# Spans of 256 steps, 384-byte packets, 64x64 array tiles and weights prepared among the attention steps in a gated linear attention + MoE kernel

## Chip, cores, metric

One core of one Trainium2 chip. The metric is the device time of one launch in microseconds (us); lower is better.

## The reference, cut

```python
# attention: B=4, H=8, S=768, D=48
f = 1 / (1 + exp(-f_logit))
for t in range(S):
    state = f[:, :, t, :, None] * state + einsum('bhd,bhe->bhde', k[:, :, t], v[:, :, t])
    y[:, :, t] = einsum('bhd,bhde->bhe', q[:, :, t], state)
# MoE: x = y as (3072 tokens, 384); w1, w2: 384 x 1024; w_out: 1024 x 384
out = maximum(x @ w1, x @ w2) @ w_out
```

Both kernels use max(a, b) = b + relu(a - b). So the output is x·(w2·w_out) + relu(x·(w1 - w2))·w_out. The matrix `m2` = w2·w_out and the difference `wd` = w1 - w2 (rows permuted) are computed once at the start on the chip. Attention is done in chunks: decays become exponentials of cumulative sums, and inside a chunk it is products of matrices.

## The kernel before

It works on tiles of 128 steps of one batch: 24 tiles, two tiles form a token group of 256 for the MoE. The stages have one-letter names, which the rest of the text uses. SBUF and PSUM are the on-chip memories in which the tiles lie (results of TensorE land in a bank of PSUM), and a semaphore is the counter by which one engine waits for another:

| letter | engine | what |
|---|---|---|
| E | ScalarE | `ell` = ln(1 + exp(-f)) |
| C, X | TensorE, ScalarE | cumulative sums `cum`; exponentials `f_inv`, `f_dec`, `f_last` |
| M, V | GpSimd (or VectorE) | k' = k·f_inv (`kp`), q' = q·f_dec (`qp`); v to bf16 (`vb`) |
| T | TensorE, VectorE | transposes of k', q' (`trp`), copied to SBUF (`trs`) |
| A | TensorE, VectorE | scores (`at`), masked (`at_m`) |
| S, Y | TensorE, ScalarE | y from the state, y from the scores (`y`), copied to `xT` |
| D, N | TensorE, VectorE, GpSimd | sums for the next state (`sadd`) and the new state |
| d | TensorE, ScalarE | h = x·wd (24 matmuls), relu to `gT` |
| o | TensorE, VectorE | x·m2 + gT·w_out (22 matmuls), out |

```python
def load(n, names="fkqv"):                       # 192-byte packets: 48 floats
    t = inp.tile([C, H, D], F32, ...)
    nc.sync.dma_start(out=t, in_=sources[nm][b, :, c*C:(c+1)*C, :].rearrange("h p d -> p h d"))
def stage_T_pe(n):                               # 8 transposes, 128x128
    for x, nm in enumerate(("kp", "qp")):
        for j in range(NP):
            nc.tensor.transpose(out=ps[:, x, j, :], in_=src[:, 2*j:2*j+2, :]..., identity=ident)
def stage_A_pe(n):                               # 8 products on two row halves of the array
    for j in range(NP):
        for r in range(2):
            rows = slice(r*DP, r*DP + D)
            nc.tensor.matmul(out=ps[r][:, j, :], lhsT=t[rows, 0, j, :], rhs=t[rows, 1, j, :], ...)
# ... start: tiles 0-3, then weights, wd ahead of the first d, m2 behind it ...
while n < n_tiles + 2 or queue["d"] or queue["o"]:
    do("A", n); do("Y", n - 1); do("C", n + 2); do("M", n + 2); next_piece("d", n)
    do("V", n + 1); do("T", n + 1); next_piece("d", n); do("E", n + 3); next_piece("o", n)
    n += 1
# ... cut: constants, stages E, C, X, M, V, Y, D, pieces d and o, weights
```

## Time and profile before

| | before |
|---|---|
| time, median (lowest to highest of the runs beside the new kernel) | 175.56 us (174.80 to 175.78) |
| span in the profile | 173.1 us |
| TensorE busy / idle | 140.5 / 32.6 us |
| mean granted clock of TensorE | 0.99 |
| first h matmul | 37.26 us |
| one round of 128 steps, steady | 5.05 us (10.1 per 256) |

"Busy" is the time in which an engine executes; idle is the span less busy. The granted clock says at what share of full speed TensorE was allowed to run. The lines of this profile that carry the argument stand in the prediction; two more from its page's slices (40 equal parts of the span) are needed later, the granted clock in tenths and the transfer rate in GB/s:

```profile
PEclk9999999999699999999999999999999999999999
GB/s 116 195 215 399 399 290 183 202 187 186 188 179 7 95 81 206 132 156 195 139 210 179 188 233 194 214 168 233 212 189 220 157 155 45 57 49 57 45 95 93
```

There is one dip of the clock. (The trace's record of the clock begins at 37.3 us, and what lies before is counted as full; the weight matmuls just before, 512 columns each, start 0.43 us apart, against 0.23 in e6, so TensorE ran at about half clock there too. The new kernel's record begins at 15.2 us, that of its repeat at 31.3. So means of the clock over whole runs are not quite comparable; the stretches after the first h are.) Where DMA is busy with the 192-byte input packets, it moves around 190 GB/s; the 399 are the weights.

### The profile page before, as it was taken

The page shows a single profiled execution, that of the slowest core. Times are in us where ns is not written, and L with a number is a line of the kernel's source. Part 1 is how long each engine was busy: PE and PEld are TensorE (multiplying, and loading weights), DVE is VectorE, ACT ScalarE, POOL GpSimd, SP SyncE. Part 2 cuts the span into 40 slices and gives each one's busy share as a digit, 9 for nine tenths or more (in the row PEclk, how much of TensorE's full clock was granted, in tenths as well). Part 3 has the DMA queues.
Part 4 walks back from the last instruction along what each step waited for, and adds up shares of the span by engine and source line. Part 5 has one row for each costly group of instructions (what it writes and reads, how often), then busy time and mean ns, then how long its engine had stood idle before and what let it go on. Part 6 is the DMA issues. An engine that isn't in the chain of part 4 may idle for free.

```text
span 173.1 us, 4159 instructions
## 1 busy us (share of the span) xinstructions
PE 140.5 (81%) x1636; PEld 97.8 (56%) x1637; DVE 88.4 (51%) x168; ACT 94.4 (55%) x205; POOL 64.4 (37%) x79
## 2 busy tenths in 40 slices
PE   0157461694969958699999999999999999999992
PEld 0034250252436647567777777777777777766760
DVE  8119239410058976555467655556765554542121
ACT  4263570159234676966848396684949665343410
POOL 2078008700004465636535345652634564000000
PEclk9999999999699999999999999999999999999999
DMA  6999999999990449689799899979989741111122
GB/s 116 195 215 399 399 290 183 202 187 186 188 179 7 95 81 206 132 156 195 139 210 179 188 233 194 214 168 233 212 189 220 157 155 45 57 49 57 45 95 93
DMA packets 106772, 29.18 MB, mean 169 GB/s; under 512 B 100736, under 2 KB 105984, under 8 KB 106752
## 3 DMA queue, kind: packets, MB, share of 16 engines
q1 hardware_dynamic: 105216, 28.32, 80.6%
q10 hardware_dynamic: 1536, 0.59, 1.5%
q8 instruction: 13, 0.21, 0.5%
q14 instruction: 7, 0.06, 0.1%
HBM read 23.59 MB, written 4.72 MB: 164 GB/s over the span
## 4 chain that ended last, share of the span: by engine, by line
PE 66%; DMA 9%; DVE 8%; ACT 6%; SPq 6%; issue 2%; ACTq 1%
PE h L275 18%; PE o L285 17%; PE o L282 6%; DMA kt<-in_k_dram 5%; SPq L71 5%; PE trp L176 4%; PE at_e L194 4%; PE y L221 4%; PE y L216 3%; DMA w_f<-in_moe_w_dram 3%; PE wdp L312 3%; PE m2n L326 3%; DVE wdn L305 3%; PE cum L143 3%; ACT wo L322 2%
## 5 line engine op out<-in xcount | busy, mean ns | idle before, releaser
L163 POOL TENSOR_TENSOR kp<-kt,f_inv 128x384 bf16<-128x384 f32 x24 | 26.0, 1082 | 51.0 <-ACT f_inv L156 40.3
L275 PE MATMUL h<-xT,wd 128*128 128x256 bf16 x288 | 38.1, 272 | 0.1
L285 PE MATMUL o<-wo,gT 128*128 128x384 bf16 x192 | 35.1, 326 | 0.0
L288 DVE COPY ob<-o 128x384 f32<-128x384 f32 x24 | 13.3, 556 | 41.6 <-PE o L285 41.6
L277 ACT ACTIVATE gT<-h 128x512 bf16<-128x512 f32 x48 | 28.0, 610 | 8.9 <-PE h L275 8.5
L275 PEld LDWEIGHTS <-wd 128*128 128x128 bf16 x288 | 25.9, 98 | 3.9 <-issue 1.0
L260 ACT CAST xT<-y 128x512 bf16<-128x512 f32 x24 | 14.0, 583 | 22.0 <-PE y L221 21.8
L285 PEld LDWEIGHTS <-gT 128*128 128x128 bf16 x192 | 18.8, 98 | 12.4
L165 POOL TENSOR_TENSOR qp<-qt,f_dec 128x384 bf16<-128x384 f32 x24 | 25.0, 1043 | 0.1
L184 DVE COPY trs<-trp 128x1024 bf16<-128x1024 bf16 x24 | 16.5, 688 | 12.3 <-PE trp L176 12.3
L251 POOL TENSOR_TENSOR state<-tmp_s,f_last 128x256 bf16<-128x256 f32 x16 | 10.6, 662 | 29.8 <-DVE tmp_s L250 24.7
L156 ACT ACTIVATE f_inv<-cum 128x384 f32<-128x384 f32 x24 | 11.8, 491 | 16.7 <-POOL state L251 8.1
L202 DVE TENSOR_TENSOR at_m<-at_e,ut 128x512 bf16<-128x512 f32 x24 | 16.4, 682 | 2.0 <-PE at_o L194 2.0
L143 PE MATMUL cum<-ell,ut 128*128 128x384 bf16 x24 | 8.6, 359 | 10.6 <-ACT ell L137 10.6
L202 DVE TENSOR_TENSOR at_m<-at_o,ut 128x512 bf16<-128x512 f32 x24 | 16.3, 679 | 0.0
L136 ACT ACTIVATE tmp_e<-ft 128x384 f32<-128x384 f32 x24 | 12.8, 532 | 6.4 <-DMA ft<-in_f_logit_dram 6.4
L282 PE MATMUL o<-m,xT 128*128 128x384 bf16 x72 | 15.6, 326 | 0.0
L194 PE MATMUL at_e<-trs 48*128 48x128 bf16 x96 | 9.9, 226 | 4.0 <-DVE trs L184 3.7
L137 ACT ACTIVATE ell<-tmp_e 128x384 bf16<-128x384 f32 x24 | 12.6, 523 | 0.8
L169 DVE CAST vb<-vt 128x384 bf16<-128x384 f32 x24 | 11.4, 475 | 2.6 <-DMA vt<-in_v_dram 2.6
L146 PEld LDWEIGHTS <-ell 128*128 128x128 bf16 x96 | 6.1, 100 | 11.1 <-issue 9.8
L194 PEld LDWEIGHTS <-trs 48*128 48x128 bf16 x192 | 5.7, 97 | 11.2 <-DVE trs L184 5.9
(51 smaller groups left out, 178.0 us busy)
## 6 DMA issues: line engine op xcount, KB each, us to landing
ft<-in_f_logit_dram SPq DMA_DIRECT2D x24, 192.0 KB, 4.1
kt<-in_k_dram SPq DMA_DIRECT2D x24, 192.0 KB, 4.6
qt<-in_q_dram SPq DMA_DIRECT2D x24, 192.0 KB, 4.6
vt<-in_v_dram SPq DMA_DIRECT2D x24, 192.0 KB, 4.2
out_dram<-ob SPq DMA_DIRECT2D x24, 192.0 KB, 3.0
w_f<-in_moe_w_dram SPq DMA_DIRECT2D x6, 512.0 KB, 6.1
wo_f<-in_moe_w_out_dram SPq DMA_DIRECT2D x2, 768.0 KB, 9.2
xT<-xT ACTq DMA_DIRECT2D x24, 24.0 KB, 3.6
```

What stands on the lines that cost most here:

```text
L143: nc.tensor.matmul(out=ps[:, 0:HD].rearrange("p (h d) -> p h d", h=H), lhsT=ut, rhs=ell[:, :, 0:D], start=True, stop=True)
L163: nc.gpsimd.tensor_mul(padded["kp"][n % NB][:, :, 0:D], loaded[n]["k"], f_inv.rearrange("p (h d) -> p h d", h=H))
L165: nc.gpsimd.tensor_mul(padded["qp"][n % NB][:, :, 0:D], loaded[n]["q"], f_dec.rearrange("p (h d) -> p h d", h=H))
L184: nc.vector.tensor_copy(t, ps)
L194: nc.tensor.matmul(out=ps[r][:, j, :], lhsT=t[rows, 0, j, :], rhs=t[rows, 1, j, :], start=True, stop=True)
L202: nc.vector.tensor_mul(m[:, r], ps[r], ut4)
L260: nc.scalar.copy(xT[g][:, :, b * C:(b + 1) * C], ys.pop(n))
L275: nc.tensor.matmul(out=ps[:, f, :], lhsT=wd[:, kt, ff * C:(ff + 1) * C], rhs=xT[g][:, kt, :], start=(kt == 0), stop=(kt == KT - 1))
L277: nc.scalar.activation(gT[g][:, 2 * fp:2 * fp + 2, :], ps, AF.Relu)
L282: nc.tensor.matmul(out=ps, lhsT=xT[g][:, kt, b * C:(b + 1) * C], rhs=m2[:, kt, :], start=(kt == 0), stop=False)
L285: nc.tensor.matmul(out=ps, lhsT=gT[g][:, ff, b * C:(b + 1) * C], rhs=wo[:, ff, :], start=False, stop=(ff == FG - 1))
L288: nc.vector.tensor_copy(ob, ps)
```

## The change

The intent: half as many packets of twice the size, attention products that fill all four 64x64 quarters of the array, and TensorE kept busy at the start by attention work while weights arrive. A span is now 256 steps with steps 2p and 2p+1 on partition p; one span is one token group. The diff, cut to its core:

```diff
-            t = inp.tile([C, H, D], F32, name=f"{nm}t", tag=f"{nm}t")
-            nc.sync.dma_start(out=t, in_=...[b, :, c * C:(c + 1) * C, :].rearrange("h p d -> p h d"))
+            t = inp.tile([C, H, 2, D], F32, name=f"{nm}t", tag=f"{nm}t", bufs=in_bufs[nm])
+            src = ...[b, :, w * W:(w + 1) * W, :].rearrange("h (p two) d -> p h (two d)", two=2)
@@ transposes: 64 small ones per span in place of 16
+                for par in range(2):
+                    for r in range(2):
+                        for h in range(2):
+                            rows = slice(h * HC, (h + 1) * HC)
+                            nc.tensor.transpose(out=ps[h][r * DP:(r + 1) * DP, x, j, par, :],
+                                                in_=src[rows, par, 2 * j + r, :], identity=ident[rows, rows])
@@ scores, state sums, y: same four-quarter loops (32, 32, 32 small matmuls); one drain and semaphore
+            nc.tensor.drain().then_inc(s_sem, 1)      # between y from the state and y from the scores
@@ order of the start
+    do("AD", 0) ... weights_w2(0); do("Y", 0); weights_w2(1); do("DAN", 1); weights_w2(2); weights_wo()
+    do("S", 1); weights_m2(); do("Y", 1)
+    weights_wd()                                   # w1 - w2 on VectorE only here
@@ order of spans 2 to 6, the ramp into the regular rounds
+    do("E", 2); do("d", 0); do("CXM", 2); do("E", 3); do("o", 0); do("VT", 2); do("d", 1)
+    do("DAN", 2); do("CXM", 3); do("E", 4); do("o", 1); do("VT", 3); do("CXM", 4)
+    do("S", 2); do("D", 3); do("Y", 2); do("AN", 3); do("E", 5); do("VT", 4); do("CXM", 5); do("E", 6)
@@ regular round
+    for s in range(4, n_s + 2):
+        T(s+1) S(s-1) D(s) Y(s-1) A,N(s) d(s-2) C,X,M(s+2) V(s+1) E(s+3) C,X,M(s+3) E(s+4) o(s-2)
```

(`do` runs a stage once, so in later rounds only what is left of the list is issued: C, X, M of span s+3, E of s+4.)

## The prediction

> **What bounds the kernel now.** I read the page first, then the chain of waits in order of time, then the timeline of one round in the steady part, then that of the start. The busy table and the slices:
>
> ```profile
> PE 140.5 (81%) x1636; PEld 97.8 (56%) x1637; DVE 88.4 (51%) x168; ACT 94.4 (55%) x205; POOL 64.4 (37%) x79
> ...
> PE   0157461694969958699999999999999999999992
> ...
> DMA  6999999999990449689799899979989741111122
> ```
>
> TensorE is full from about 65 us on, and half empty before. DMA is busy nearly everywhere too, but the chain from 77.6 us on consists of TensorE alone. The busy table of the stretches says the same:
>
> ```profile
> 36.00:50.00 14.00, 10.99 (x59) 6.36 (x58) 1.20 (x3) 8.02 (x12) 0.00 (x0) 0.88 1.42 187
> 50.00:78.00 28.00, 22.70 (x351) 16.75 (x350) 21.08 (x40) 17.54 (x43) 13.91 (x15) 1.00 0.60 116
> ...
> 77.60:153.00 75.40, 75.35 (x990) 55.16 (x989) 44.82 (x89) 48.98 (x114) 35.69 (x41) 1.00 0.84 172
> ```
>
> So 75.35 of 75.40 us are TensorE: transfers are hidden there, and only TensorE time counts. It takes 5.05 us per 128 steps. Where they go, from the timeline of one such round:
>
> ```profile
> 102.15 0.41 PE L221 MATMUL y<-at_m,vb 128*64 128x128 bf16 x8
> 102.40 0.29 PE L234 MATMUL sadd<-vb,kp 128*64 128x64 bf16 x8
> 102.62 0.34 PE L143 MATMUL cum<-ell,ut 128*128 128x384 bf16 x1
> 102.80 0.24 PE L146 MATMUL cum<-ones_col,ell 128*128 128x1 bf16 x4
> 102.90 0.82 PE L275 MATMUL h<-xT,wd 128*128 128x256 bf16 x6
> 103.55 0.39 PE L176 MATMUL trp<-ident,kp 128*128 128x128 bf16 x4
> 103.78 0.39 PE L176 MATMUL trp<-ident,qp 128*128 128x128 bf16 x4
> 104.00 0.82 PE L275 MATMUL h<-xT,wd 128*128 128x256 bf16 x6
> 104.66 0.65 PE L282 MATMUL o<-m,xT 128*128 128x384 bf16 x3
> 105.14 1.46 PE L285 MATMUL o<-wo,gT 128*128 128x384 bf16 x8
> 106.54 0.23 PE L194 MATMUL at_e<-trs 48*128 48x128 bf16 x1
> ```
>
> Matmuls overlap, so I take distances between starts: h 12 x 0.109 = 1.31, o 11 x 0.163 = 1.79, together 3.1 us that the change leaves alone; cum 0.28, transposes 0.45, the scores A (to 106.87) 0.33, y from the state (to 107.21) 0.34, y from the scores 0.24, sadd 0.22: attention 1.86 us.
>
> The start, from the timeline: the first h matmul is at 37.26 us, after the subtraction w1 - w2 (26.62 to 31.7) and twelve matmuls at 0.43; m2 is ready at 51; the regular rounds begin there and still lose 5.3 us (28.0 - 22.7) before 78.
>
> **What the Trainium skill says.** "TensorEngine Tiling (Array Packing)", Key Properties: changing the tiling mode drains TensorE. The trace agrees: eight score matmuls in pairs 56 ns apart need 0.22 us but the next group starts after 0.33; eight sadd at 13.6 ns are 0.11 but cum starts after 0.22. About 0.11 us per change, four changes in a round. "TensorE: Matmul & The Clock Gate", Part 3: tiles in different row or column groups overlap, starting about 4 ns apart. The trace shows pairs only: the two score halves start within 10 ns. No run yet shows four at once. The same page, Part 1: an idle window of about 3.4 us puts the clock back to half. The trace fits: m2n matmuls run 0.32 us apart after an idle stretch, though the equally long o ones take 0.163. "DMA: Bandwidth & Descriptors", Specifications: line rate needs 512 B or more. Packet medians in this trace: 192 B 15 ns, 512 B 27, 4096 B 159, so about 8.2 ns plus 0.0368 ns per byte; 384 B come to an estimated 22.3 ns.
>
> **Part 1, packets.** Inputs are 18.9 MB. Before: 98304 packets x 15.2 / 16 engines = 93 us of transfer; after: 49152 x 22.3 / 16 = 68.5. The gain of 25 us lies beside a full TensorE, so it is worth nothing in the steady part. At the start two spans (3.15 MB) take 11.4 us at 275 GB/s where 1.57 MB took nearly 8, so weights still end near 25 us. Value by itself: about zero.
>
> **Part 2, 64x64 tiles, per 256 steps.** Before: 2 x 1.86 = 3.72. After, if four tiles run at once (four of 128 columns per 56 ns, four of 64 per 27 to 28): transposes 64 = 16 x 0.028 = 0.45 (0.90 before); state product 16 on the two diagonal tiles, 8 x 0.056 = 0.45; state sums 32 = 0.22; y from scores 32 = 0.45; scores 32 = 0.45. Products and sums take the array time they took. cum grows: four matmuls of 384 columns in place of two, 0.65, and eight of two columns at 0.025, 0.20, sum 0.85. Mode changes fall from eight to two, plus one explicit drain with its semaphore: 0.4 in place of 0.9. Sum 3.27; MoE is still 6.2; a span takes 9.5 us against 10.1. Some nine steady spans: 5 to 6 us won. The other engines fit below 9.5: ScalarE, by distances of starts (384 columns 0.375, 512 0.5): E 1.7, X 1.7, y copies 1.05, relu 2.1, two DMA issues 1.2 = 7.8; VectorE 6.2; GpSimd 4 x 0.95 + 2 x 0.66 = 5.1.
>
> **Part 3, the start.** I followed the instruction order of the new kernel by hand. f of span 0 lands at 3.9, E0 to 5.65, cum (half clock) to 7.5, exponentials to 9.2; k' on GpSimd and q' on VectorE share time (w1 - w2 took 2.01 us per part beside GpSimd, 1.21 alone), to 11; transposes, cum of span 1, scores, masks to 16.9 on VectorE; q' of span 1 after them, to 18.2; its transposes 18.7; y of span 0 to 21.3; then on ScalarE in order: copy of y and DMA issues to 23.6, two w2 casts to 25.6, two wo casts to 28.5. So m2n can start at 28.5 and is done about 33.5, m2 at 35.6. Only then does VectorE subtract w1 - w2 (3 x 1.2, to 39.2), with TensorE idle; thirteen wd matmuls, at first cold, end near 43.5. The first h comes **6 us later** than before, but with m2 and two spans (four old tiles) finished.
>
> **Part 4, the ramp.** A span's chain from cum to transposes is long: exponentials 0.9, then 2 x 1.9 on GpSimd, 5.1 us with the cum. Where the new order puts little on TensorE between, it waits: before the transposes of span 2 (o of 3.6 us between) 1.8, of span 3 1.0, of span 4 2.4, of span 5 (straight behind its cum, which itself waits for E) 5, and before cum 7, behind exponentials 6 and E7, 3.7. Near 14; I take 13, as some of the distances are pessimistic.
>
> **The sum.** 43.5 to the first h; MoE 12 x 6.2 = 74.4; attention of ten spans 10 x 3.3 = 33; stalls 13; last copy and 384 KB out 4 (3.3 for 192 KB before): 167.9 us of span. The time is 2.7 above the span (175.76 - 173.1): **170.6 us**, 3% faster.
>
> **Rivals.** (a) *Issue of small tiles becomes the bound.* TensorE gets 2781 matmuls in place of 1636. The fastest sustained start distance seen is 13.6 ns (sadd). If that is a floor per instruction rather than two tiles sharing, transposes take 0.85 and sums 0.43: +0.6 a span, all gain of part 2 gone, 177 us. For it: every matmul has its own weight load. Against it: loads and matmuls in the trace start two at a time, then pause 27 ns, as tile time would make them. (b) *The ramp swallows it.* If k' and q' are slowed by VectorE, as at 26 to 32 us before, each wait grows by 1 to 2 us, idle gaps above 3.4 us halve the clock, and the time is 174 to 176. (c) *The start is better than my chain.* If m2n runs at full clock and the wd preparation overlaps more, h comes at 38 to 39 and the time is near 165. (d) *Transfers bound the old kernel more than I think.* DMA share 0.84 while TensorE is full speaks against it; then 25 us would come off, which I don't expect.
>
> **Range and chances.** The steady part is safe to about +-3 us unless (a) holds; start and ramp each to +-4. An order this hand-laid was probably arranged to avoid some waits I see, which pulls down; (a) and (b) pull up. Range 163.5 to 177.0. Faster by over 2% means below 172.2, only 1.6 above my figure: 0.60; within 2% 0.34; slower 0.06.
>
> **What would show it.** Right: steady spans of 9.4 to 9.6 us with TensorE full; transposes of a span in 0.5 us; first h near 43; idle TensorE before the transposes of span 5 and cum 7; DMA share near 0.6 in the steady part. Wrong: transposes near 0.9 us (rival a); TensorE waiting for VectorE or GpSimd in every span (then an engine that I count as having slack sets the pace); first h before 39 (rival c); a steady span above 10 us.

## The result and the profile after

| | before | after |
|---|---|---|
| time, median (range), 4 runs each | 175.56 (174.80 to 175.78) | 181.24 (180.59 to 182.09) |
| span in the profile | 173.1 | 179.0 |
| TensorE busy + idle | 140.5 + 32.6 | 140.3 + 38.7 |
| mean granted clock, as recorded | 0.99 | 0.91 (four runs: 0.89 to 0.94) |
| first h | 37.26 | 43.37 |
| 256 steps, steady | 10.1 | 9.73 |

The ratio is 1.033 (95%: 1.028 to 1.039): the new kernel is slower. A ratio here is the mean time of one kernel's fast runs over that of the other's fast runs of the same rounds, so it isn't quite the ratio of the medians in the table.

The new kernel's page: busy times, and the slices of TensorE, clock, DMA and rate.

```profile
PE 140.3 (78%) x2780; PEld 99.5 (56%) x2781; DVE 90.0 (50%) x168; ACT 88.5 (49%) x169; POOL 55.8 (31%) x56
...
PE   0355649839979664379299999999999999999990
...
PEclk9999557987999997556969999999999999999999
DMA  6999999999039499999553959620202020202022
GB/s 150 261 261 379 378 383 244 265 261 254 13 93 277 112 268 242 239 273 209 145 120 97 267 154 241 163 98 4 101 2 93 15 95 11 96 8 97 2 92 88
```

Each digit is 4.5 us. From the 21st digit on (90 us) TensorE is full, as planned. Before it there is a hole of seven digits, and under most of it the clock reads 5 to 7. DMA is nearly idle in the last third. The busy table by stretch (length, then busy time and number of instructions of TensorE, its weight loads, VectorE, ScalarE, GpSimd; then granted clock, DMA share, GB/s; the share adds up packet times, which overlap, so it can exceed 1):

```profile
43.37:64.07 20.70, 16.94 (x310) 11.99 (x308) 9.13 (x15) 12.95 (x25) 8.05 (x5) 1.00 0.60 138
64.07:75.45 11.38, 5.85 (x201) 4.17 (x192) 6.44 (x11) 7.14 (x16) 6.33 (x5) 0.75 1.09 250
...
81.00:95.31 14.31, 10.85 (x70) 6.64 (x68) 3.24 (x7) 8.98 (x19) 8.01 (x5) 0.79 0.64 140
95.31:124.50 29.19, 28.75 (x703) 21.73 (x702) 18.06 (x33) 18.78 (x39) 13.83 (x12) 1.00 0.59 157
```

The last line is three regular rounds: 28.75 of 29.19 us busy at full clock. From the first h to there, 51.94 us, TensorE idles 14.0 us, and for half of the time after 64 us it runs at half clock. One regular round, as the timeline shows it (start, duration of the group, engine, line, operands, count):

```profile
105.05 0.45 PE L218 MATMUL trp<-ident,kp 64*64 64x64 bf16 x32
105.32 0.43 PE L218 MATMUL trp<-ident,qp 64*64 64x64 bf16 x32
...
106.60 0.64 PE L295 MATMUL y<-at_m,vb 64*64 64x128 bf16 x32
107.07 0.62 PE L235 MATMUL at<-trs 48*64 48x128 bf16 x32
107.63 2.79 PE L349 MATMUL h<-xT,wd 128*128 128x256 bf16 x24
...
111.11 0.65 PE L359 MATMUL o<-m,xT 128*128 128x384 bf16 x3
...
114.78 0.41 PE L218 MATMUL trp<-ident,kp 64*64 64x64 bf16 x28
```

Distances of starts (the lines left out start the state product at 105.57 and cum at 110.26): transposes 0.52, state product, sums and drain 1.03, y 0.47, scores 0.56, h 2.63, cum 0.85, o 3.67; sum 9.73. The 64 small transposes take little more than half of what 16 large ones took (0.90). And the waits of TensorE from the first h to the regular rounds (sum, times, longest):

```profile
PE trp L218 <- POOL qp L201: 4.2, 4, 1.6
PE cum L175 <- ACT ell L166: 3.9, 2, 3.5
PE trp L218 <- POOL kp L201: 3.8, 2, 2.9
```

So the tiles work and the start comes when predicted. Where did the time go? Busy plus idle says: 5.9 us more span are 6.1 us more idle and 0.2 us less busy. That last figure is a sum of two: the experiments below (e1, e7) show the same instructions at 136.0 us busy when the clock stays up. So about 4.5 us of work were removed as hoped, and 4.3 us came back, most of it as half clock.

When did the clock drop? The changes of clock lie on a grid of 3.41 us. The busy table cut on that grid:

```profile
66.40:69.81 3.41, 1.43 (x75) 0.92 (x63) 3.07 (x6) 2.12 (x6) 3.41 (x3) 1.00 1.21 249
69.81:73.22 3.41, 2.27 (x44) 1.47 (x44) 1.65 (x3) 1.59 (x4) 0.83 (x1) 0.50 0.99 246
...
86.87:90.29 3.42, 1.17 (x14) 0.78 (x14) 0.00 (x0) 2.25 (x6) 3.41 (x2) 1.00 1.05 247
```

After a window with 1.43 us of work, and again after one with 1.17, the next runs at half clock (the last column but two; 90.29 to 93.70 reads 0.50 like the second line). The waits need not be long each: in the first of these windows none is over 0.89 us. And half clock does not last for one window alone: the windows from 69.81 us on, with 2.27, 0.64 and 2.69 us of work, were each followed by another at half clock, and only after the one with 3.41 us (80.05 to 83.46) was it full again.

### The profile page after: what moved, and what is told of

Same layout as the page of the kernel before. It is cut to its first block, busy times and chain, and to the rows that moved or that the text cites. A ratio compares the mean times of both kernels' runs of the same rounds, so it can differ in the third digit from the quotient of the medians.

```text
span 179.0 us, 6262 instructions
## 1 busy us (share of the span) xinstructions
PE 140.3 (78%) x2780; PEld 99.5 (56%) x2781; DVE 90.0 (50%) x168; ACT 88.5 (49%) x169; POOL 55.8 (31%) x56
## 4 chain that ended last, share of the span: by engine, by line
PEld 17%; issue 15%; ACT 11%; PE 9%; ACTq 5%; POOL 4%; PEldq 3%; DVE 0%; POOLq 0%
ACT gT L351 7%; PEld L362 6%; ACTq L336 5%; ACT xT L333 3%; POOL qp L201 3%; PE o L362 3%; PEld L349 3%; PE y L295 3%; PEldq L256 3%; PEld L218 2%; PEld L276 2%; PEld L359 2%; PE h L349 1%; PE at L235 1%; PE o L359 1%
## 5 line engine op out<-in xcount | busy, mean ns | idle before, releaser
L201 POOL TENSOR_TENSOR kp<-kt,f_inv 128x768 bf16<-128x768 f32 x12 | 21.8, 1813 | 42.4 <-ACT f_inv L193 39.9
L247 DVE TENSOR_TENSOR at_m<-at,mask 128x512 bf16<-128x512 f32 x48 | 29.8, 684 | 2.9 <-PE at L235 2.4
L333 ACT CAST xT<-y 128x512 bf16<-128x512 f32 x24 | 12.9, 593 | 32.6 <-PE y L295 32.6
L175 PE MATMUL cum<-ell,u_inc 128*128 128x384 bf16 x36 | 11.3, 372 | 10.4 <-ACT ell L166 10.2
L201 POOL TENSOR_TENSOR qp<-qt,f_dec 128x768 bf16<-128x768 f32 x10 | 18.5, 1846 | 0.0
L218 PE MATMUL trp<-ident,kp 64*64 64x64 bf16 x384 | 5.9, 203 | 9.7 <-POOL kp L201 8.1
L165 ACT ACTIVATE tmp_e<-ft 128x768 f32<-128x768 f32 x12 | 10.6, 880 | 4.8 <-DMA ft<-in_f_logit_dram 3.5
L193 ACT ACTIVATE f_dec<-cum 128x384 f32<-128x384 f32 x24 | 10.8, 523 | 0.0
L166 ACT ACTIVATE ell<-tmp_e 128x768 bf16<-128x768 f32 x12 | 10.1, 843 | 0.4
L218 PE MATMUL trp<-ident,qp 64*64 64x64 bf16 x384 | 5.9, 206 | 5.5 <-POOL qp L201 4.2
L295 PE MATMUL y<-at_m,vb 64*64 64x128 bf16 x384 | 8.5, 234 | 1.5 <-PEq L256 0.2
```

The costliest lines, as they stand in the source:

```text
L193: nc.scalar.activation(t[:, pt, :], ps[pt][:, 0:HD], AF.Exp, bias=0.0, scale=scale)
L201: eng.tensor_mul(pad(nm + "p", s)[:, :, :, 0:D], by_parity(loaded[s][nm]), t.rearrange("p two (h d) -> p two h d", h=H))
L218: nc.tensor.transpose(out=ps[h][r * DP:(r + 1) * DP, x, j, par, :], in_=src[rows, par, 2 * j + r, :], identity=ident[rows, rows])
L247: nc.vector.tensor_mul(m[:, r, 2 * jj:2 * jj + 2], ps[r], mask.rearrange("p j a b t -> p j a (b t)"))
L295: nc.tensor.matmul(out=ys[s][h][r * DP:(r + 1) * DP, j, :], lhsT=vb[rows, par, 2 * j + r, :], rhs=m[rows, r, j, par, :], start=first, stop ...
L333: nc.scalar.copy(x[:, :, :, h, :], ps.rearrange("p j (a t) -> p j a t", a=2))
```

## The experiments

All twelve gave correct results. Theory "ramp": the loss lies in the order of the start and of spans 2 to 7, which leaves TensorE waiting and so also lowers its clock; tiles, packets and spans are sound. Rival "tiles": the small tiles are slower than the large ones they replaced. Rival "packets": they don't help, or the loads of 384 KB come too late. Ratios are to the kernel before on the same chip. "After" had 1.033 in its first runs. Medians are of all four runs; e1, e2 and e5 have one slow run each and e8 has two, which the ratios leave out.

| run | what | median us (range) | ratio (95%) |
|---|---|---|---|
| e1 | new order of the ramp | 167.73 (166.36 to 169.37) | 0.951 (0.948 to 0.955) |
| e2 | unread work in the longest gap | 181.45 (180.57 to 184.18) | 1.034 (1.029 to 1.039) |
| e3 | large transposes | 184.96 (183.76 to 186.51) | 1.056 (1.049 to 1.063) |
| e4 | 192-byte packets | 185.70 (184.14 to 186.59) | 1.059 (1.052 to 1.065) |
| after again | unaltered | 182.32 (180.11 to 182.77) | 1.040 (1.033 to 1.047) |
| e5 | unread work in two gaps | 182.70 (182.06 to 185.50) | 1.044 (1.038 to 1.049) |
| e6 | w1 - w2 earlier | 177.22 (176.92 to 177.43) | 1.013 (1.009 to 1.018) |
| e7 | e1 + e6 | 164.08 (163.16 to 165.20) | 0.939 (0.933 to 0.945) |
| e8 | e7, E of span 7 later | 162.52 (160.74 to 164.21) | 0.917 (0.913 to 0.922) |
| e9 | e7 with large transposes | 164.65 (164.25 to 165.66) | 0.939 (0.935 to 0.944) |
| e10 | e7 with 192-byte packets | 181.05 (180.39 to 182.26) | 1.032 (1.027 to 1.037) |
| e11 | 100 unread instructions early | 187.79 (one run) | none |

### e1: the order of the ramp

```diff
-    do("S", 1); weights_m2(); do("Y", 1); weights_wd(); do("E", 2); do("d", 0)
-    do("CXM", 2); do("E", 3); do("o", 0); do("VT", 2); do("d", 1); do("DAN", 2); do("CXM", 3); do("E", 4)
-    do("o", 1); do("VT", 3); do("CXM", 4); do("S", 2); do("D", 3); do("Y", 2); do("AN", 3)
-    do("E", 5); do("VT", 4); do("CXM", 5); do("E", 6)
+    do("S", 1); do("E", 2); weights_m2(); do("CX", 2); do("Y", 1); weights_wd()
+    stage_M(2, nc.vector); do("V", 2); do("E", 3); do("d", 0); do("CXM", 3); do("T", 2); do("o", 0)
+    do("E", 4); do("DAN", 2); do("CXM", 4); do("VT", 3); do("d", 1); do("E", 5)
+    do("S", 2); do("D", 3); do("Y", 2); do("AN", 3); do("CXM", 5)
+    do("o", 1); do("VT", 4); do("E", 6); do("CXM", 6); do("E", 7)
```

> The changed kernel with the order of spans 2 to 7 in the ramp rearranged only: E, cum and exponentials of a span, and its products, are issued a stage earlier (those of span 2 before the wd preparation, those of 3 behind d0, cum 7 one round later), so that o or d of another group lies between a span's cum and its transposes. Theory 'ramp': TensorE idle between first h and the first regular round falls from 14 us to 3 to 6, the clock stays near 1.0 there (before: 0.5 to 0.8 in three stretches, some 5 us), so 8 to 14 us less than the changed kernel, 167 to 173. Rival 'tiles' (the small matmuls are the loss) and rival 'start' (first h 6 us later): the time hardly moves, under 3 us.

Measured: 167.73 us, 7.5 below the kernel before of the same rounds and 13.5 below the new kernel's median. Besides the order, one thing was changed: q' of span 2 is computed by VectorE (0.95 us) in place of GpSimd. Its page, then its busy table from the first h to 85 us:

```profile
PE   0336719981999969669999999999998999999990
...
PEclk9999999999699999999999999999999999999999
```

```profile
45.87:85.00 39.13, 34.13 (x906) 24.73 (x905) 24.55 (x42) 27.43 (x56) 21.24 (x15) 1.00 0.81 192
```

The hole is gone, the clock stays at 1.00 through the whole ramp. Busy falls from 140.3 to 136.0 us, idle from 38.7 to 30.6. This happens though the first h is 2.5 us later (45.87): GpSimd's k' of span 2 now falls beside the subtraction w1 - w2 on VectorE, whose last part takes 2.83 us in place of 1.22; that is 1.6 of the 2.5 us. Theory "ramp" holds: the order, with that one product moved, is worth more than the whole loss.

### e2: work without use in the longest gap

```diff
+            if s == 7 and pt == 0:
+                for _ in range(20):
+                    nc.tensor.matmul(out=ps[:, 0:HD], lhsT=u_inc, rhs=wo[:, 0, :], start=True, stop=True)
```

> The changed kernel with twenty matmuls of 384 columns that nobody reads put before cum 7, where TensorE sits idle 3.5 us. They take 3.2 us at full clock and so fit in the gap. Theory 'clock' (the idle gap halves the clock for the work behind it: o of group 2 took 5.1 us in place of 3.6): useless work makes the kernel 1 to 2 us faster, and the o matmuls behind it start 0.163 us apart. Rival (those o matmuls are slow for another reason, e.g. they wait for ScalarE): no change, or slower by what the filler delays.

The gap of 3.46 us before cum 7 is filled with 20 matmuls that nobody reads, to keep the clock up without ending the wait. The o matmuls of group 2 after the gap, in the new kernel and in e2:

```profile
89.97 0.84 PE L359 MATMUL o<-m,xT 128*128 128x384 bf16 x3
90.61 2.77 PE L362 MATMUL o<-wo,gT 128*128 128x384 bf16 x8
...
95.31 0.45 PE L218 MATMUL trp<-ident,kp 64*64 64x64 bf16 x32
```

```profile
90.99 0.65 PE L362 MATMUL o<-m,xT 128*128 128x384 bf16 x3
91.48 1.46 PE L365 MATMUL o<-wo,gT 128*128 128x384 bf16 x8
...
94.66 0.45 PE L221 MATMUL trp<-ident,kp 64*64 64x64 bf16 x32
```

They take 3.67 us (90.99 to 94.66) instead of 5.34: the drop of the clock was caused by the gap, and costs 1.7 us here. But the whole did not become faster (1.034 against 1.033). The profiled run was a slow one, so I don't compare its span; in it TensorE stands still later, for 0.74 us in the next h and for 1.26 us in the scores of a steady span at 138.22, where no semaphore explains it, and the clock drops once more after the second. What these pauses are, e11 shows.

### e3: the transposes back in 128x128

```diff
-                    for r in range(2):
-                        for h in range(2):
-                            nc.tensor.transpose(out=ps[h][r * DP:(r + 1) * DP, x, j, par, :], in_=src[rows, par, 2 * j + r, :], ...)
+                    nc.tensor.transpose(out=ps[:, j, par, :], in_=src[:, par, 2 * j:2 * j + 2, :]..., identity=ident)
+            for h in range(2):
+                nc.vector.tensor_copy(t[:, h, x], ps[:, :, :, h * HC:(h + 1) * HC])
```

> The changed kernel with the transposes alone done as before, 16 of 128x128 a span in place of 64 of 64x64, and four copies of half the width out of them. Theory 'tiles help': transposes go from 0.53 to about 0.95 us a span, a steady span from 9.73 to 10.1, the whole 2 to 4 us slower than the changed kernel. Rival 'tiles are the loss' (the number of small instructions): faster than the changed kernel by 2 us or more.

Slower, 1.056: by 1.5 to 2.2% against the two sets of runs of the new kernel. The steady round takes 10.12 us (from h to h) in place of 9.73; some eight such rounds make 3.1 us. Rival "tiles" falls: in the steady part the small ones are the better ones, by 0.39 us a span.

### e4: back to 192-byte packets

```diff
-            nc.sync.dma_start(out=t.rearrange("p h two d -> p h (two d)"), in_=src)
+            for two in range(2):
+                nc.sync.dma_start(out=t[:, :, two, :], in_=src[:, :, two, :])
```

> The changed kernel with each input load split in two by parity, which gives back 192-byte packets and twice the issues; layout and all else stay. If transfers are hidden behind TensorE in the steady part: steady spans stay at 9.7 us, DMA share there rises from about 0.6 to 0.85; only the start moves, f of span 1 lands about 3 us later and the whole is 1 to 4 us slower. Rival 'the packets are worth the whole gain of the steady part': spans of 10 us or more and over 6 us slower.

Slower, 1.059; the median is 3.4 to 4.5 us over those of the new kernel's two sets; the first h comes at 47.51 in place of 43.37, the steady round stays at 9.73. So the packets matter in the start alone, with this order. The prediction had put their value there at "about zero", which was wrong.

### after again: the new kernel unaltered

> The changed kernel again, unaltered, as the base for its neighbours on the same chip: 180 to 182 us, mean granted clock 0.89 to 0.95.

182.32 us, ratio 1.040; recorded clocks of its four runs 0.95, 0.93, 0.93, 0.89. The result holds. The runs scatter by 1.5%. The two profiled runs of this kernel have equally much half clock after the first h (17.1 us) and differ by one window before it: the first ran at half clock from 39.1 to 42.5 us, this one at full, and its first h comes 0.45 us earlier. Whether the rest of the scatter is of this kind isn't shown.

### e5: both gaps filled

```diff
+        if s == 5:      # ahead of the transposes of span 5; e2's 20 matmuls stay
+            pre[3] = bank("y0")
+            for _ in range(8):
+                nc.tensor.matmul(out=pre[3][:, 0:HD], lhsT=u_inc, rhs=wo[:, 0, :], start=True, stop=True)
```

> The changed kernel with useless matmuls in two gaps: eight of 384 columns before the transposes of span 5 (about 2.6 us at half clock, in a wait of 2.9) and the twenty before cum 7 of the run before. Theory 'clock': TensorE keeps or regains its full clock before d of group 2, so d and o of groups 2 run at 0.109 and 0.163 us apart, and some 3 us come off the changed kernel run beside it (177 to 179). Rival (the clock costs nothing that ScalarE or GpSimd would not cost anyhow): within 1 us of it.

A miss: 182.70, not faster than the new kernel on the same chip (182.32). By the number, the rival of the expectation came true. In its profile (again a slow run, so only single durations are read) the transposes of span 5, the products after them and h of group 2 do run at full clock. But the clock had dropped two windows earlier (63.1 us), and drops again at 100.6 us, so the half clock after the first h is 17.1 us as before: the filling moved it and did not shorten it. And h stops:

```profile
81.27 0.93 PE L359 MATMUL h<-xT,wd 128*128 128x256 bf16 x7
84.69 1.05 PE L359 MATMUL h<-xT,wd 128*128 128x256 bf16 x8 [2.50 <-issue]
```

2.50 us in which TensorE waited for nothing that the profile names ("issue"). There was one such pause in the new kernel too, in the transposes of span 4:

```profile
68.03 0.26 PE L218 MATMUL trp<-ident,kp 64*64 64x64 bf16 x8 [0.69 <-DVE at_m L247]
69.18 0.38 PE L218 MATMUL trp<-ident,kp 64*64 64x64 bf16 x24 [0.89 <-issue]
```

I looked up which TensorE instruction of the program each such pause stands before. New kernel: row 1724 (its repeat and e6 pause there too, for 1.04 and 0.67 us). e5: 2234, and a second pause at 2744. e2: 2742 (the matmul's own weight load is the row before it). They are 510 rows apart, wherever in the work that falls. And in the trace's transfers of the instruction queue (22 packets of 16 KB for the 5,561 matmuls and weight loads of TensorE, 253 each; 13 in the kernel before, which has no such pause after its first h) a packet landed 1.3 to 1.7 us before TensorE went on: 67.84 and 69.18 in the new kernel, 83.03 and 84.69 in e5. So a second theory, "supply": TensorE had run out of instructions, because the next block came late. A span's five attention groups are 352 instructions in 2.6 us. That full DMA engines delay the block is not shown: in e2 they carried nothing from 132.0 to 135.6 us, and the packet for the pause at 138.22 started at 135.62 only. The packets of these runs took 0.9 to 1.9 us each.

### e6: w1 - w2 ahead of the products for m2

```diff
     do("S", 1)
+    weights_wdn()      # the three VectorE subtractions, until now the first lines of weights_wd
     weights_m2()
```

> The changed kernel with one move: VectorE subtracts w1 - w2 before it copies m2, not after. In the changed kernel TensorE idles 3.3 us for that subtraction and VectorE had waited for m2 since about 30 us. Theory 'start order': the subtraction ends near 34 us in place of 38.8, the first h comes at 38 to 39 in place of 43.4, and the whole is 4 to 6 us faster than the changed kernel, 175 to 177: the start costs as much as its place in the chain says, and the ramp's waits stay as they are. Rival (the start is covered by the ramp: what is won is waited for again): under 2 us.

177.22, 5.1 below the unaltered kernel of the same rounds; first h 39.11 in place of 42.92. The subtraction waited behind VectorE's m2 copies for no reason of data. 3.8 of the 5.1 us are the earlier first h.

### e7: both orders

```diff
+    do("E", 2); weights_wdn()      # e6's line, ahead of weights_m2; the rest is e1's order
     weights_m2(); do("CX", 2); do("Y", 1); weights_wd(); stage_M(2, nc.vector); ...
```

> Both orders together: the ramp of the first run and the early subtraction. In the first run the subtraction took 5.1 us beside a GpSimd product and put the first h to 45.9 us; now it should be over before that product starts. If the two costs are separate, first h at 39 to 40, and 5 to 6 us come off the 167.7 of the first run: 161 to 164. If the ramp then waits for input or ScalarE instead, 165 to 168.

164.08, 6.1% below the kernel before. First h 41.27, busy 136.1, idle 27.3 us. Its remaining waits in the ramp: 1.04 and 1.80 us for E of spans 5 and 6, and 2.2 us within h of group 2. The window around the last has 1.19 us of work, and the next ran at half clock.

### e8: E of span 7 later

```diff
     do("CXM", 6)
-    do("E", 7)
...
         do("V", s + 1)
+        if s == 4:
+            do("o", g)
         do("E", s + 3)
```

> Both orders together, with E of span 7 moved behind the copy of y of span 3 and behind o of group 2. In the run before, ScalarE stood in front of that E until 69.0 us for its input, kept the copy of y waiting until 70.7, and TensorE sat 2.2 us in d of group 2 for a bank. If that wait is separate, it is gone and 1.5 to 3 us come off 164.1: 161 to 163. If the next wait takes its place: 163 to 165.

162.52; the two runs that count as fast give 161.51 and 160.74, ratio 0.917, the lowest of all. But the pause in h of group 2 that it was to end is still there (2.55 us, at the same row 2232, in a slow run's profile), so I can't say that the gain over e7 comes from where I sought it. The four runs fall in two pairs 2.7 us apart, and only the faster pair enters the ratio; with all four the median is 0.925 of that of the kernel before.

### e9: large transposes in the good order

```diff
-    64 transposes of 64x64 per span, 2 copies (e7)
+    16 transposes of 128x128 per span, 4 copies of half the width (e3's stage_T, on e7)
```

> Both orders together with 16 transposes of 128x128 a span. The steady span was 10.12 in place of 9.73 us with them in the changed kernel. If the tiles' gain is there where the ramp doesn't hide it: some 0.4 us times seven to nine spans, 3 to 4 us slower than both orders alone (167 to 168). If the small instructions cost more in the full ramp than they save: no slower.

A miss: 164.65 and ratio 0.939, the same as e7. The steady round is longer as in e3 (10.06 to 10.12), but its h of group 3 starts at 78.61 where e7's starts at 82.05. The 2.2 us pause within h of group 2 is absent: with 5,132 instructions in place of 6,259 that h lies elsewhere in the program (rows 1644 to 1690, where e7 has 2220 to 2266). What the tiles win in the steady part is lost in the ramp. "Supply" fits this, though a second wait could be at work: in e7 the row of the pause is also the first of a new PSUM bank for h, and the profile names VectorE there, in e8 ScalarE. For "supply" speaks that in all four runs with small tiles in this order (e1, e7, e8, e10) TensorE goes on there 1.3 to 1.7 us after a packet of its instruction queue landed.

### e10: 192-byte packets in the good order

```diff
-            nc.sync.dma_start(out=t.rearrange("p h two d -> p h (two d)"), in_=src)
+            for two in range(2):
+                nc.sync.dma_start(out=t[:, :, two, :], in_=src[:, :, two, :])      # on e7
```

> Both orders together with 192-byte packets. In the changed kernel they cost 4 us at the start and nothing in the steady part. Now the ramp uses input faster (transfer share 0.99 from 40 to 72 us), so they should cost more: 4 us at the start and 4 to 8 in the ramp, 171 to 176, near the kernel before. If only the start counts: 168.

181.05, 17 us slower than e7, more than I expected. Its DMA slices, with e7's spans, tiles and order but the old packets:

```profile
DMA  5999999999999999999899898999902020202022
GB/s 107 199 191 188 330 379 385 179 199 185 192 155 170 222 170 157 193 166 179 222 206 176 169 214 172 206 204 191 248 17 99 9 97 9 97 6 98 1 92 88
```

DMA is full until slice 29 (130 us) at around 190 GB/s. As the ramp runs earlier, inputs are wanted earlier, and at that rate they can't come. So the packets, worth 3.4 to 4.5 us in the order as given, are worth 17 us once the order is good. (The edit also doubles the number of load instructions, as the kernel before has them; the full DMA slices speak for the packets.)

### e11: moving the rows

```diff
+            if kt == 0:        # ahead of m2n
+                for _ in range(50):
+                    nc.tensor.matmul(out=ps[:, 0:64], lhsT=u_inc, rhs=wo[:, 0, 0:64], start=True, stop=True)
```

> The changed kernel with fifty small matmuls that nobody reads (100 instructions of TensorE with their loads) in the idle stretch before m2n. Two runs with fillers showed pauses of TensorE that no semaphore explains; counted in instructions they lie at 1724, 2234 and 2744, always 510 apart, and each comes 1.3 to 1.7 us after a 16 KB packet of the instruction queue has landed. Theory 'instruction supply': here too the pauses fall on the instructions counted 1724 or a multiple of 255 away from it, which are now 100 places earlier in the program; the pause inside the transposes of span 4 is no longer behind its eighth matmul. Rival (a wait that belongs to those transposes): it stays behind the eighth. The whole changes by under 2 us.

50 unread matmuls with their weight loads move every later instruction by 100 rows. If pauses belong to the work, they stay in the transposes of span 4; if they belong to the program's rows, they move to other work. They moved:

```profile
65.22 0.52 PE L295 MATMUL y<-at_m,vb 64*64 64x128 bf16 x22 [0.17 <-PEq L256]
66.08 0.36 PE L295 MATMUL y<-at_m,vb 64*64 64x128 bf16 x10 [0.34 <-issue]
```

```profile
99.97 0.34 PE L235 MATMUL at<-trs 48*64 48x128 bf16 x10
101.78 0.52 PE L235 MATMUL at<-trs 48*64 48x128 bf16 x22 [1.48 <-issue]
```

The transposes of span 4 have no pause now. The 23rd y matmul of the first pair is row 1724; the 11th score matmul of the second is row 2744; and between them the second score matmul of span 4 waits 0.55 us, row 2234 (there the profile names ScalarE). The same three rows as before, in other work, each 1.4 to 1.5 us after a packet of the instruction queue landed; and a fourth, 1.75 us in the scores of the next span (113.78), lies 508 rows further, 1.5 us after its packet. "Supply" is shown for these pauses. The whole was 6 us slower, where I expected under 2. It is a single run of unknown state, but its trace accounts for most of it: the four pauses are 4.1 us where the new kernel has 0.9, and after the first h it runs 23.9 us at half clock in place of 17.1, an estimated 3.4 us of lost time. So where the pauses fall can cost several us, and again through the clock.

## Why the prediction was wrong

I predicted 170.6 us (163.5 to 177.0) and gave "slower" 0.06. It is 181.24.

**The steady part: right, slightly mis-sized.** 9.5 us a span predicted, 9.73 measured; transposes 0.52 (0.45), scores 0.56 (0.45), y 0.47 (0.45), cum 0.85 (0.85), MoE 6.30 (6.2). The 6.2 was short by the prediction's own lines: o runs from 104.66 to 106.54, 1.88 us and not 1.79, and its items add up to 4.96 of the 5.05 us of a round. TensorE is full there as predicted. Rival (a), issue of small tiles as the bound, is refuted by the halved transposes and by e3. In the span's sum these sizes cost 1.2 + 1.3 = 2.5 us: 12 x 6.30 for 12 x 6.2, and 10 x 3.43 for 10 x 3.3.

**The start: right.** First h at 43.37, predicted 43.5, with the chain as described: the subtraction comes behind the m2 copies. I took this delay as given; e6 shows that it was a needless 3.8 us.

**The waits of the ramp: right.** Predicted before the transposes of spans 2 to 5: 1.8, 1.0, 2.4, 5 and 3.7 before cum 7, "near 14; I take 13". Measured 1.25, 2.5, 1.8, 4.5 and 3.46, all idle 14.0. The sum is better than its parts, and that is luck: span 3 was too low by 1.5 us and the others were too high. Part of the 1.8 is the pause of instruction supply (0.89), which I did not foresee.

**The sum: this is the step that failed.** It added the waits to work at full clock: "stalls 13". The same text says in rival (b) that such gaps halve the clock, and then leaves it out of the sum and holds it for the less likely case. With the waits as predicted it was no rival but the consequence of my own step. Measured piece by piece at half clock: S, D, Y, A of spans 3 and 4 in 3.05 us for 2.06, h of group 2 in 3.95 for 2.63, o of group 2 in 5.34 for 3.67, and cum 5 with the transposes of spans 4 and 5 some 1.1 more: about 5.1 us. By e1's busy time it is 4.3. No run changed the clock alone for the whole (e2 and e5 only moved its drops), so the size rests on these durations and on e1, which removed most of the waits and all of the half clock after the first h together. A second term was missing too: each wait also exposes the last 0.2 us of the matmul before it, which distances between starts hide; twelve waits make an estimated 2.4.

Filled in, the sum closes: 43.4 + 75.6 + 34.3 + 14.0 + 4.0 = 171.3, with the half clock 5.1 and the exposed ends 2.4 = 178.8, against a span of 179.0. So of the 11.1 us by which the span was mis-sized, the half clock is 5.1, the steady sizes 2.5, the exposed ends 2.4 and the waits 1.0. The time lies 1.8 over the span, not 2.7: the prediction set the median of 175.76 against the span of an execution that took 174.97.

**The packets: wrong.** "Value by itself: about zero" holds only for the steady part. e4 shows 3.4 to 4.5 us in the given order, e10 17 us in a better one. A 384-byte packet took 25 ns in the median, not the estimated 22.3. The error did not move the prediction, as both kernels were weighed with their own packets at the start.

**The chances: too sure.** "Arranged to avoid some waits I see" was a hope against my own reading of the order. None of the waits was avoided. A gain of 0.6 us a span over some nine spans (as measured 9 x 0.37 = 3.3 us) could not pay for 6 us at the start and 14 us of waits; the kernel before loses only 5.3 us in its ramp after 50 us.

What stays open: how much the supply of instructions costs the whole, in the new kernel (0.89 us are seen) and in e7; what makes a block of instructions late; and why e8 is faster than e7.

## What to carry to other kernels

When a change brings waits of a few microseconds to TensorE, count them twice: once as idle time, once as half clock for the work that follows, by cutting the busy table into windows of 3.41 us and looking for those under half full; the half clock then lasts until a window that is nearly full (four windows here, from 69.81 to 83.46 us). Judge a redesign apart from the order in which it is first issued: here almost the same instructions ran in 181 us and, reordered, in 164 us (e7), and the worth of the parts changed with the order: the packets went from some 4 us to 17, the transposes in 64x64 from about 3 us to nothing. Pauses that no semaphore explains, at fixed distances in the program, point to the instruction supply; here they came with small tiles, whose instructions are short.

## What the Trainium skill lacked or had wrong

- "Runtime: NRT & Kernel Launch", Instruction fetch mechanics, says that crossing a 16 KiB block of 256 instructions is mostly hidden, since instructions are dispatched slower than they are fetched. Here TensorE in 64x64 tiles used 352 instructions in 2.6 us (7.4 ns each), and it paused 0.3 to 2.5 us at rows 1724, 2234 and 2744, until 1.3 to 1.7 us after a 16 KB packet of its instruction queue had landed (new kernel, e2, e5, e11). The page doesn't say what can make the packet late, and no run here shows it.
- "TensorE: Matmul & The Clock Gate", Part 1, has the clock fall after an idle window of about 3.4 us; further down it has drops from frequent short idles too, but with no limit. The grid of 3.41 us is seen here, and the window need not be idle: 1.43 and 1.17 us of work in it were followed by half clock, while 1.61 us (59.6 to 63.0 us) kept the full one. The limit is not the same everywhere (in e3 1.80 us did not keep it). Nor did every busy window bring the clock back (2.69 us did not, 3.41 did).
- "TensorEngine Tiling (Array Packing)", Key Properties, names the drain at a change of mode without a cost: about 0.11 us in the kernel before (0.33 us to the next group for 0.22 us of score matmuls).
- "DMA: Bandwidth & Descriptors", Specifications, gives only the limit of 512 B, and the page's account of small packets has no rate for these sizes. By the slices in which DMA was full: around 190 GB/s with packets of 192 B, 261 with 384 B, 380 to 400 with the weights' 4096 B. Below the limit the size still decides.
